# Retention in front of two expert layers: row stores on ScalarE's queue, eight load buffers, query scaling ahead of key scaling, and the first tile's turn behind the second tile's scores

## The chip, the cores and the metric

The kernel runs on one core of a Trainium2 chip, as one program. The metric is the device time of one execution in microseconds, and the time of a kernel is the median of its runs. The profiles are made by the hardware profiler during one execution.

## What is computed

Three layers follow each other, all in float32. The first is retention: causal scores with a decay for each head, no softmax. The second routes each of 2304 tokens to one of 8 experts with a fixed capacity, in the order of the logits over all tokens and experts. The third is a dense layer whose gate is h * tanh(softplus(h)).

```python
scores = scale * np.matmul(q, k.transpose(0, 1, 3, 2))      # 4 batches, 8 heads, 576 rows, 64
ret = scores * Dmat[None, :, :, :]                          # gamma[h] ** (i - j) below the diagonal
x = np.matmul(ret, v)                                       # -> 2304 rows x 512
logits = x @ w_gate
for idx in np.argsort(-logits.flatten()):                   # greedy, capacity 2304 // 8 a expert
...
out[mask] = np.maximum(x[mask] @ w1[e], 0.0) @ w2[e]
h = out @ w_in
g = h * np.tanh(np.log1p(np.exp(np.minimum(h, 20.0))))
return g @ w_out
```

## The kernel before

**Retention** (`attention`, lines 133 to 334) goes through 18 tiles of 128 rows, four and a half tiles a batch. It computes the sum over earlier rows in chunks: within a tile by masked scores, between tiles by a running state of 64 x 64 a head. For each tile t there are seven steps, each a small function:

- `load` (L163) brings two blocks of 512 KB from HBM: `qk` (queries and keys, transposed) and `kv` (keys and values by rows). It is issued on SP's queue into the pool `ld`, which has six buffers of each.
- `scale` (L175) makes `ks` (keys times decay, L181) and then `qs` (queries times decay, L185), on GpSimd (POOL), but for tile 0, whose `ks` VectorE makes. In tiles 4 and 13, where a new batch begins in mid-tile, `qs` is a kept tile `qz`.
- `scores` (L187): 16 matmuls into two of three PSUM banks, then VectorE multiplies by the mask (`am`, L198).
- `carried` (L214): the product of state `S` and `qs` (L223) into the bank pair `pT`.
- `outputs` (L226): values times masked scores (L232) into the same pair; ScalarE (ACT) copies it to `xT` in two halves (L236).
- `state` (L200): adds `ks` times values to the running state in PSUM (L209); VectorE makes `S` for the next tile (L212).
- `turn` (L238): TensorE (PE) transposes `xT` against a tile that holds the identity and the gate's weights (L246), so that rows and logits come out together; VectorE adds up the logits `L` (L248), ACT copies the rows to `xs` (L250), and a DMA on SP's queue stores them to the scratch tensor `x` (L252), 256 KB a tile.

The order of PE, VectorE and POOL is the order in which the code is written (`manual_schedule`, L147). SP's and ACT's instructions are put in order by the framework's scheduler. It also gives each DMA of SP's and ACT's queues one of eight counters, `DMAHW0` to `DMAHW7`, in turn; a DMA waits, before it is issued, until the last DMA on its own counter has landed.

The first two tiles are written by hand (L278 to L294): scores(0), then for tile 0 carried, outputs, state, turn, scores(1), and for tile 1 scores(2), carried, outputs, state, turn, state(2). The loop from L295 takes two tiles o and b = o + 1 a round: scores(b), carried(o), carried(b), scores(b + 1), the scaling of the tiles two to four ahead, outputs(o), state(b), outputs(b), state(b + 1), turn(o), turn(b). When the last logits are there, routing begins with the counts `pF` (L331).

**After retention**, an order of work planned by `run_tasks` (L715) covers the rest: routing finds one expert after the other with its tokens by a search over the logits' bits, SP loads that expert's weights by the number found (`eid`), POOL gathers its rows of `x` by indirect DMA (L646), PE runs the expert (L810), and the dense layer follows in six tiles of 384 tokens (L1033, L1094). Nothing of this is touched by the change.

Of the kernel before, what the change touches and what calls it, by code (L numbers as in the profile page):

```python
# [7 lines left out]
F32 = mybir.dt.float32  # L8
# [5 lines left out]
ALU = mybir.AluOpType  # L14
# [3 lines left out]
P = 128  # L18
B, H, S, D = 4, 8, 576, 64
# [109 lines left out]
class Kernel:  # L129
# [3 lines left out]
    def attention(self):  # L133
        tc, nc, a = self.tc, self.nc, self.a
# [5 lines left out]
        self.ident = persist.tile([P, P], F32, name="ident")  # L140
        self.L = L = persist.tile([P, NT, E], F32, name="L")
        with ExitStack() as st:
            ld = st.enter_context(tc.tile_pool(name="ld", bufs=6))
            wk = st.enter_context(tc.tile_pool(name="wk", bufs=4))
            one = st.enter_context(tc.tile_pool(name="one", bufs=1))
            ps = st.enter_context(tc.tile_pool(name="ps", bufs=1, space=PSUM))
# [4 lines left out]
            gks = dec[:, DC["gk"]].rearrange("p (t h) -> p t h", h=H)  # L151
# [9 lines left out]
            QK, KV, QS, KS, AM, XT, PT, Sb = {}, {}, {}, {}, {}, {}, {}, {}  # L161
# [10 lines left out]
            def starts(t):  # L172
                return (t * P) % S == 0

            def scale(t, eng, keys=True, queries=True):  # L175

                if t >= NT:
                    return
                if keys and not starts(t + 1):
                    KS[t] = wk.tile([P, H, D], F32, name="ks")  # L180
                    eng.tensor_tensor(KS[t], KV[t][:, 0], gks[:, t, :, None].to_broadcast([P, H, D]), op=ALU.mult)  # L181
                if queries and not starts(t):
                    n = 64 if t in STRADDLE else P
                    QS[t] = QZ[t] if t in STRADDLE else wk.tile([P, HP, P], F32, name="qs")
                    eng.tensor_tensor(QS[t][:, :, :n], QK[t][:, 0, :, :n], gqs.rearrange("p (h i) -> p h i", i=P)[:, :, :n], op=ALU.mult)  # L185

            def scores(t):  # L187
                if t >= NT:
                    return
                into = [pA[(2 * t + i) % 3] for i in range(2)]  # L190
                for hp in range(HP):
                    for i in range(2):
                        sl = slice(i * 64, i * 64 + 64)
                        for o in (slice(0, 64), slice(64, P)):
                            nc.tensor.matmul(into[i][o, hp, :], QK[t][sl, 1, hp, o], QK[t][sl, 0, hp, :], start=True, stop=True)
                AM[t] = wk.tile([P, 2, HP, P], F32, name="am")
                for i in range(2):
                    nc.vector.tensor_tensor(AM[t][:, i], into[i], masks[t in STRADDLE][:, i], op=ALU.mult)  # L198

            def state(t):  # L200

                if starts(t + 1):
                    return
                s1 = ((t + 1) * P - 1) % S
                begin = s1 < P
                lo = P - 1 - s1 if begin else 0
                for h in range(H):
                    o = slice(h % 2 * 64, h % 2 * 64 + 64)
                    nc.tensor.matmul(pS[o, h // 2, :], KS[t][lo:, h, :], KV[t][lo:, 1, h, :],  # L209
                                     start=(begin and h < 2), stop=False, skip_group_check=True)  # L210
                Sb[t + 1] = wk.tile([P, HP, D], F32, name="S")
                nc.vector.tensor_tensor(Sb[t + 1], pS, gss[:, t + 1, :, None].to_broadcast([P, HP, D]), op=ALU.mult)  # L212

            def carried(t):  # L214

                PT[t] = ps.tile([P, 2, 512], F32, name="pT", bufs=2)[:, :, :2 * P].rearrange("p i (k j) -> p i k j", k=2)
                if starts(t):
                    return
                for k in range(2):
                    for i in range(2):  # L220
                        sl = slice(i * 64, i * 64 + 64)
                        for q in range(2):
                            nc.tensor.matmul(PT[t][q * 64:q * 64 + 64, i, k, :], Sb[t][sl, 2 * k + q, :], QS[t][sl, 2 * k + q, :],  # L223
                                             start=(k == 0), stop=False, skip_group_check=True)

            def outputs(t):  # L226

                first = starts(t)
                for i in range(2):
                    for k in range(2):  # L230
                        for q in range(2):
                            nc.tensor.matmul(PT[t][q * 64:q * 64 + 64, i, k, :], KV[t][:, 1, 4 * k + 2 * q + i, :], AM[t][:, i, 2 * k + q, :],  # L232
                                             start=(first and k == 0), stop=(k == 1), skip_group_check=True)
                XT[t] = wk.tile([P, HP, P], F32, name="xT")
                for i in range(2):
                    nc.scalar.copy(XT[t][:, 2 * i:2 * i + 2], PT[t][:, i])  # L236

            def turn(t):  # L238

                if t < 0:  # L240
                    return
                xs = wk.tile([P, DM], F32, name="xs")
                pX = ps.tile([P, 2, 512], F32, name="pX", tag="pT", bufs=2)
                for i in range(2):
                    for k in range(2):
                        nc.tensor.matmul(pX[:, i, k * P:k * P + P + E], XT[t][:, 2 * i + k, :], both[:, i, E - k * E:P + 2 * E - k * E],  # L246
                                         start=(k == 0), stop=(k == 1), skip_group_check=True)
                nc.vector.tensor_reduce(L[:, t, :], pX[:, :, P:P + E].rearrange("p i e -> p e i"), AX.X, ALU.add)  # L248
                for i in range(2):
                    nc.scalar.copy(xs.rearrange("p (k q i d) -> p i k q d", q=2, i=2, d=D)[:, i],  # L250
                                   pX[:, i, :2 * P + 2 * E].rearrange("p (k c) -> p k c", k=2)[:, :, :P].rearrange("p k (q d) -> p k q d", d=D))
                nc.sync.dma_start(a["x"][t * P:(t + 1) * P, :], xs)  # L252

            warm = one.tile([P, 512], BF16, name="warm")
            nc.vector.memset(warm, 0.0)
# [21 lines left out]
            nc.sync.dma_start(self.tri, a["tri"])  # L277
            scores(0)  # L278
            scale(0, nc.vector)
            scale(1, nc.gpsimd)  # L280
            scale(2, nc.gpsimd)
            for t in range(2):
                scale(t + 3, nc.gpsimd, queries=t == 0)
                if t:
                    scores(t + 1)
                carried(t)
                outputs(t)
                state(t)
                if t != 1:
                    turn(max(t - 1, 0))  # L290
                if t == 0:
                    scores(1)
            turn(t)
            state(t + 1)  # L294
            for o in range(2, NT, 2):  # L295
                b = o + 1
                load(o + 3)
# [25 lines left out]
            t = b  # L323
# [832 lines left out]
```

## Time and profile before

| | |
|---|---|
| time, median of 3 runs | 793.49 us (793.35 to 793.95) |
| the profiled execution | 789.16 us |
| its span, first to last instruction | 787.4 us |
| mean granted TensorE clock | 0.981 |
| PE, VectorE, POOL, ACT busy | 749.0, 671.5, 487.3, 406.1 us |
| retention, to the last instruction before the counts of routing | 0 to 83.1 us |
| bytes moved by DMA | 112.53 MB, of it 24.13 MB in the first 70 us |

The span is counted from the first to the last instruction; what lies around it, 1.8 us, belongs to the execution. The profiled execution is 4.3 us below the median of the runs. Windows and starts are in microseconds from the span's start. A DMA queue shows as SPq or ACTq: the instruction there only issues the transfer, and the landing comes later. "issue" as the reason of a wait means that the profile shows nothing for which the engine waited.

### The profile page before, as it was taken

The page shows a single profiled execution, that of the slowest core. Times are in us where ns is not written, and L with a number is a line of the kernel's source. Part 1 is how long each engine was busy: PE and PEld are TensorE (multiplying, and loading weights), DVE is VectorE, ACT ScalarE, POOL GpSimd, SP SyncE. Part 2 cuts the span into 40 slices and gives each one's busy share as a digit, 9 for nine tenths or more (in the row PEclk, how much of TensorE's full clock was granted, in tenths as well). Part 3 has the DMA queues.
Part 4 walks back from the last instruction along what each step waited for, and adds up shares of the span by engine and source line. Part 5 has one row for each costly group of instructions (what it writes and reads, how often), then busy time and mean ns, then how long its engine had stood idle before and what let it go on. Part 6 is the DMA issues. An engine that isn't in the chain of part 4 may idle for free.

```text
span 787.4 us, 16146 instructions
## 1 busy us (share of the span) xinstructions
PE 749.0 (95%) x6180; PEld 679.0 (86%) x6180; DVE 671.5 (85%) x1079; ACT 406.1 (52%) x781; POOL 487.3 (62%) x408
## 2 busy tenths in 40 slices
PE   7999479999999999899999999999999999999996
PEld 5889338999998999899988899899899899899894
DVE  3444787989888888777999999989999998999993
ACT  2223115657566575757764465556555545545442
POOL 5552036879798797430577586557656756756554
PEclk9999779999999999899999999999999999999999
DMA  9993165889888888986500011011001101000001
GB/s 341 406 397 117 46 215 192 272 278 306 273 299 274 288 293 265 342 290 210 174 22 21 1 51 30 1 41 31 11 1 51 31 1 41 21 1 27 14 1 40
DMA packets 61405, 112.53 MB, mean 143 GB/s; under 512 B 4880, under 2 KB 33296, under 8 KB 61328
## 3 DMA queue, kind: packets, MB, share of 16 engines
q1 hardware_dynamic: 45104, 74.01, 27.5%
q10 hardware_dynamic: 13248, 28.06, 10.4%
q0 software_dynamic: 2976, 9.44, 3.6%
q8 instruction: 48, 0.79, 0.4%
q14 instruction: 29, 0.24, 0.1%
HBM read 88.94 MB, written 22.54 MB: 142 GB/s over the span
## 4 chain that ended last, share of the span: by engine, by line
PE 38%; DVE 17%; POOL 3%; DMA 2%; issue 2%; ACT 2%; POOLq 0%; SPq 0%; ACTq 0%; DVEq 0%
PE mmc L1033 15%; PE po L1094 15%; DVE q L1063 9%; DVE n L1058 5%; PE mma L810 4%; PE mmb L810 3%; DVE n L1068 2%; DMA st<-w 1%; ACT whi L597 1%; POOL gl L1075 1%; DVE wlo L600 1%; POOL n L1065 1%; DMA q<-y_scratch 1%; POOL out L1108 1%; DMA yt<-y_scratch 0%
## 5 line engine op out<-in xcount | busy, mean ns | idle before, releaser
L1063 DVE RECIPROCAL q<-q 128x384 f32<-128x384 f32 x96 | 243.8, 2540 | 0.0
L1065 POOL TENSOR_TENSOR n<-n,q 128x384 f32<-128x384 f32 x96 | 100.9, 1051 | 161.6 <-DVE q L1063 153.7
L600 POOL TENSOR_TENSOR wlo<-st,whi 128x1024 fp32r<-128x1024 f32 x51 | 122.6, 2417 | 16.5 <-ACT whi L597 12.2
L1033 PE MATMUL mmc<-yh,whi 128*128 128x384 f32 x384 | 129.9, 338 | 0.8 <-DVE n L1068 0.8
L1033 PE MATMUL mmc<-yh,wlo 128*128 128x384 f32 x384 | 129.9, 338 | 0.0
L1033 PE MATMUL mmc<-yl,whi 128*128 128x384 f32 x384 | 129.8, 338 | 0.1
L1075 POOL TENSOR_TENSOR gl<-n,gh 128x384 fp32r<-128x384 f32 x96 | 120.0, 1252 | 3.6 <-ACT gh L1073 3.5
L1073 ACT CAST gh<-n 128x384 fp32r<-128x384 f32 x96 | 49.3, 514 | 141.0 <-DVE n L1068 140.5
L1058 DVE SCALAR_TENSOR_TENSOR n<-s 128x384 f32<-128x384 f32 x96 | 114.7, 1197 | 5.1 <-POOL gl L1075 3.9
L1094 PE MATMUL po<-whi,gl 128*128 128x512 f32 x288 | 113.9, 395 | 0.7 <-POOL gl L1075 0.4
L1094 PE MATMUL po<-whi,gh 128*128 128x512 f32 x288 | 114.4, 397 | 0.2 <-ACT gh L1073 0.2
L1094 PE MATMUL po<-wlo,gh 128*128 128x512 f32 x288 | 114.1, 396 | 0.0
L597 ACT CAST whi<-st 128x1024 fp32r<-128x1024 f32 x80 | 82.7, 1044 | 33.8 <-DMA st<-w 28.1
L810 PE MATMUL mma<-xh,whi 128*128 128x288 f32 x256 | 78.5, 307 | 2.9 <-ACT xh L657 2.6
L810 PE MATMUL mma<-xl,whi 128*128 128x288 f32 x256 | 77.5, 303 | 1.7 <-DVE xl L659 1.7
L810 PE MATMUL mmb<-hl,whi 128*128 128x288 f32 x256 | 77.3, 302 | 0.0
L810 PE MATMUL mmb<-hh,whi 128*128 128x288 f32 x256 | 77.3, 302 | 0.0
L810 PE MATMUL mma<-xh,wlo 128*128 128x288 f32 x256 | 76.9, 301 | 0.0
L1033 PEld LDWEIGHTS mmc<-yh,whi 128*128 128x128 f32 x384 | 72.1, 188 | 5.2 <-DVE n L1068 1.2
L810 PE MATMUL mmb<-hh,wlo 128*128 128x288 f32 x256 | 75.9, 297 | 0.0
L1033 PEld LDWEIGHTS mmc<-yl,whi 128*128 128x128 f32 x384 | 72.1, 188 | 4.1 <-DVE yl L993 0.3
L1033 PEld LDWEIGHTS mmc<-yh,wlo 128*128 128x128 f32 x384 | 72.0, 188 | 0.0
(152 smaller groups left out, 1546.9 us busy)
## 6 DMA issues: line engine op xcount, KB each, us to landing
st<-w SPq DMA_DIRECT2D x64, 512.0 KB, 6.0
qk<-qk SPq DMA_DIRECT2D x18, 512.0 KB, 8.0
kv<-kv SPq DMA_DIRECT2D x18, 512.0 KB, 8.7
std<-w_out ACTq DMA_DIRECT2D x15, 512.0 KB, 4.9
std<-w_in ACTq DMA_DIRECT2D x14, 512.0 KB, 5.6
x_scratch<-xs SPq DMA_DIRECT2D x18, 256.0 KB, 5.6
y_scratch<-y ACTq DMA_DIRECT2D x32, 144.0 KB, 4.2
yt<-y_scratch SPq DMA_DIRECT2D x22, 192.0 KB, 2.4
```

Of the source, the lines that this page charges most:

```text
L597: self.nc.scalar.copy(dst[0], st)
L600: (self.nc.vector if lo.engine == DVE else self.nc.gpsimd).tensor_tensor(dst[1], st, dst[0].bitcast(F32), op=ALU.subtract)
L810: self.nc.tensor.matmul(bank[1][:, :CAP], al if h == 2 else ah, bl if h == 1 else bh, start=(first and j == h == 0), stop=(last and j == n ...
L1033: self.nc.tensor.matmul(bank[1][:, :TILE], (wl if h == 2 else wh)[:, c, cs], x[c][h == 1], start=(c == h == 0), stop=(c == HP - 1 and h == 2))
L1058: v.scalar_tensor_tensor(u, s, 2.0, s, op0=ALU.subtract, op1=ALU.mult)
L1063: v.reciprocal(q, q)
L1065: nc.gpsimd.tensor_tensor(u, u, q, op=ALU.mult)
L1068: v.tensor_tensor(u, u, p, op=ALU.mult)
L1073: nc.scalar.copy(gh, u)
L1075: nc.gpsimd.tensor_tensor(gl, u, gh.bitcast(F32), op=ALU.subtract)
L1094: nc.tensor.matmul(po[j], (gl if h == 2 else gh)[:, js], (wl if h == 1 else wh)[:, f % 2], start=(f == h == 0), stop=(f == DFF // P - 1 an ...
L1108: d = nc.gpsimd.indirect_dma_start(out=self.a["out"], out_offset=bass.IndirectOffsetOnAxis(ap=self.tok[:, t * 3 + j:t * 3 + j + 1], axis=0 ...
```

## The change

Four edits, all in `attention`: the pool `ld` has eight buffers of each kind; `scale` makes `qs` ahead of `ks`; the store of `xs` is issued on ACT's queue; and the first two tiles are written out with scores(1) ahead of turn(0), carried(1) ahead of scores(2), and the scaling of tile 3 ahead of tile 0's steps.

```diff
-            ld = st.enter_context(tc.tile_pool(name="ld", bufs=6))
+            ld = st.enter_context(tc.tile_pool(name="ld", bufs=8))
...
-                if keys and not starts(t + 1):
-                    KS[t] = wk.tile([P, H, D], F32, name="ks")
-                    eng.tensor_tensor(KS[t], KV[t][:, 0], gks[:, t, :, None].to_broadcast([P, H, D]), op=ALU.mult)
                 if queries and not starts(t):
                     n = 64 if t in STRADDLE else P
                     QS[t] = QZ[t] if t in STRADDLE else wk.tile([P, HP, P], F32, name="qs")
                     eng.tensor_tensor(QS[t][:, :, :n], QK[t][:, 0, :, :n], gqs.rearrange("p (h i) -> p h i", i=P)[:, :, :n], op=ALU.mult)
+                if keys and not starts(t + 1):
+                    KS[t] = wk.tile([P, H, D], F32, name="ks")
+                    eng.tensor_tensor(KS[t], KV[t][:, 0], gks[:, t, :, None].to_broadcast([P, H, D]), op=ALU.mult)
...
-                nc.sync.dma_start(a["x"][t * P:(t + 1) * P, :], xs)
+                nc.scalar.dma_start(a["x"][t * P:(t + 1) * P, :], xs)
...
-            for t in range(2):
-                scale(t + 3, nc.gpsimd, queries=t == 0)
-                if t:
-                    scores(t + 1)
-                carried(t)
-                outputs(t)
-                state(t)
-                if t != 1:
-                    turn(max(t - 1, 0))
-                if t == 0:
-                    scores(1)
-            turn(t)
-            state(t + 1)
+            scale(3, nc.gpsimd)
+            carried(0)
+            outputs(0)
+            state(0)
+            scale(4, nc.gpsimd, queries=False)
+            scores(1)
+            turn(0)
+            carried(1)
+            scores(2)
+            outputs(1)
+            state(1)
+            turn(1)
+            state(2)
```

What this makes of the engines' order is seen at three places. The numbers behind the names are those of the buffers; in brackets stand the counters for which a row waits before it is issued. On SP's queue, from the identity on: `qk_314`, `kv_316` are tile 5, `qk_318`, `kv_320` tile 6, `qk_447`, `kv_449` tile 7, `qk_451` is tile 8. Before:

```order
L275 DMA ident_65<-ident 128x128 [waits DMAHW7_49]
L277 DMA tri_157<-tri 128x128 [waits DMAHW0_49]
L167 DMA qk_314<-qk 128x1024 [waits DMAHW1_49]
L170 DMA kv_316<-kv 128x1024 [waits DMAHW2_49]
L167 DMA qk_318<-qk 128x1024 [waits DMAHW3_49,PE_49]
L367 DMA rc_643<-rconsts 128x211 [waits DMAHW4_49]
L369 DMA ic_645<-iconsts 128x194 [waits DMAHW5_49]
L170 DMA kv_320<-kv 128x1024 [waits DMAHW6_49,DVE_49,PE_49]
L252 DMA x_scratch<-xs_214 128x512 [waits DMAHW7_49,Activation_49]
L167 DMA qk_447<-qk 128x1024 [waits DMAHW0_49,PE_49,Pool_49]
L167 DMA qk_451<-qk 128x1024 [waits DMAHW1_49,PE_49,Pool_49]
```

And in the change:

```order
L275 DMA ident_65<-ident 128x128 [waits DMAHW7_49]
L277 DMA tri_157<-tri 128x128 [waits DMAHW0_49]
L167 DMA qk_314<-qk 128x1024 [waits DMAHW1_49]
L170 DMA kv_316<-kv 128x1024 [waits DMAHW2_49]
L167 DMA qk_318<-qk 128x1024 [waits DMAHW3_49]
L170 DMA kv_320<-kv 128x1024 [waits DMAHW4_49]
L167 DMA qk_447<-qk 128x1024 [waits DMAHW5_49]
L170 DMA kv_449<-kv 128x1024 [waits DMAHW6_49]
L167 DMA qk_451<-qk 128x1024 [waits DMAHW7_49,PE_49]
L367 DMA rc_643<-rconsts 128x211 [waits DMAHW0_49]
L369 DMA ic_645<-iconsts 128x194 [waits DMAHW1_49]
```

The loads of tiles 6 and 7 now wait for no engine, only for their own counter, and stand two places further ahead; `kv_320` has taken counter 4 and `qk_451` counter 7. On ACT, the first tiles before (`xT_201`, `xs_214` are tile 0, `xT_281`, `xs_294` tile 1, `xT_393` is tile 2):

```order
L236 COPY xT_201<-pT_192 128x256 [waits PE_49]
L236 COPY xT_201<-pT_192 128x256
L250 COPY xs_214<-pX_215 128x4x64 [waits DVE_49]
L250 COPY xs_214<-pX_215 128x4x64
L236 COPY xT_281<-pT_264 128x256 [waits PE_49]
L236 COPY xT_281<-pT_264 128x256
L250 COPY xs_294<-pX_295 128x4x64 [waits DVE_49]
L250 COPY xs_294<-pX_295 128x4x64
L236 COPY xT_393<-pT_341 128x256 [waits PE_49]
```

And in the change (`xs_235` is now tile 0):

```order
L236 COPY xT_201<-pT_192 128x256 [waits PE_49]
L236 COPY xT_201<-pT_192 128x256
L250 COPY xs_235<-pX_236 128x4x64 [waits DVE_49]
L250 COPY xs_235<-pX_236 128x4x64
L252 DMA x_scratch<-xs_235 128x512 [waits DMAHW4_49,Activation_49]
L236 COPY xT_281<-pT_245 128x256 [waits PE_49]
L236 COPY xT_281<-pT_245 128x256
L250 COPY xs_294<-pX_295 128x4x64 [waits DVE_49]
L250 COPY xs_294<-pX_295 128x4x64
L252 DMA x_scratch<-xs_294 128x512 [waits DMAHW7_49,Activation_49]
L236 COPY xT_393<-pT_341 128x256 [waits PE_49]
```

The stores of tiles 0 and 1 now stand in ACT's stream ahead of the next tile's `xT` copies, on counters 4 and 7; the number for which the first one waits, 48, is reached when the third DMA on counter 4 has landed (16 a DMA), and that is `kv_320`; the second one's third on counter 7 is `qk_451`. On POOL, tiles 1 to 3 in the change, where every pair has changed places (before, each `ks` stood ahead of its `qs`):

```order
L182 TENSOR_TENSOR qs_180<-qk_137,gq_82 128x512 [waits DMAHW7_49,DMAHW4_49]
L185 TENSOR_TENSOR ks_182<-kv_140,dec_81 128x512 [waits DMAHW6_49,DMAHW3_49]
L182 TENSOR_TENSOR qs_184<-qk_143,gq_82 128x512 [waits DMAHW0_49]
L185 TENSOR_TENSOR ks_186<-kv_145,dec_81 128x512 [waits DMAHW1_49]
L182 TENSOR_TENSOR qs_188<-qk_147,gq_82 128x512 [waits DMAHW2_49]
L185 TENSOR_TENSOR ks_190<-kv_149,dec_81 128x512 [waits DMAHW3_49]
```

A `qs` so waits for the `qk` load alone and no longer for the `kv` load behind it. In the change's rows L182 is the query scaling and L185 the key scaling.

## Rows read from the trace of the kernel before

**Rows 1.** The page: span.

```profile
span 787.4 us, 16146 instructions
```

**Rows 2.** Windows: length, PE, PEld, DVE, ACT, POOL busy, PE clock, DMA share, GB/s.

```profile
13.10:83.10 70.00, 66.15 (x1416) 60.78 (x1416) 33.21 (x72) 20.64 (x64) 32.35 (x30) 1.00 0.78 302
83.10:108.00 24.90, 12.06 (x157) 6.71 (x155) 18.89 (x80) 1.34 (x5) 0.00 (x0) 0.66 0.17 58
```

**Rows 3.** Waits of PE, 13 to 84 us: total, times, longest.

```profile
PE pA L195 <- issue: 1.8, 2, 1.0
PE pT L223 <- POOL qs L185: 1.2, 1, 1.2
PE pA L195 <- DMA qk<-qk: 0.9, 1, 0.9
PE pT L232 <- issue: 0.6, 1, 0.6
```

**Rows 4.** Timeline of PE: turn(1), and the first counts of routing.

```profile
16.19 1.20 PE L246 MATMUL pX<-both,xT 128*128 128x136 f32 x8
...
83.11 0.53 PE L331 MATMUL pF<-oh,G 128*128 128x8 bf16 x15
```

**Rows 5.** Timeline of SP's queue, 17.5 to 27 us: issues.

```profile
18.32 0.33 SPq L167 DMA_DIRECT2D qk<-qk  x1
19.53 0.33 SPq L367 DMA_DIRECT2D rc<-rconsts  x1
...
22.20 0.33 SPq L170 DMA_DIRECT2D kv<-kv  x1
```

**Rows 6.** DMA issues, 18.2 to 19 us: size, microseconds to landing.

```profile
qk<-qk SPq DMA_DIRECT2D x1, 512.0 KB, 8.1
```

**Rows 7.** DMA, 20 to 50 us: packets, bytes, rate.

```profile
DMA packets 4265, 12.28 MB, mean 409 GB/s; under 512 B 476, under 2 KB 890, under 8 KB 4260
```

**Rows 8.** Tile kv, all its loads.

```profile
DMA to landing us min/median/max: 4.4/8.7/10.9
```

**Rows 9.** Timeline of ACT, 8.9 to 18.2 us: start, length, what, idle before.

```profile
11.43 0.65 ACT L250 COPY xs<-pX 128x256 f32<-128x256 f32 x2 [1.80 <-DVE L L248]
15.77 0.65 ACT L236 COPY xT<-pT 128x256 f32<-128x256 f32 x2 [3.69 <-PE pT L232]
```

**Rows 10.** Timeline of ACT, 144.5 to 146 us: a store's issue.

```profile
144.68 0.33 ACTq L846 DMA_DIRECT2D y_scratch<-y  x1
```

**Rows 11.** Timeline of ACT, 68.8 to 71 us: a round's second row copy.

```profile
69.91 0.65 ACT L250 COPY xs<-pX 128x256 f32<-128x256 f32 x2 [0.28 <-ACT xs L250]
```

**Rows 12.** Windows of PE: length, busy, granted clock, DMA share, GB/s.

```profile
85.00:87.90 2.90, 0.20 (x2) 1.00 0.38 143
87.90:100.90 13.00, 4.07 (x96) 0.50 0.00 1
100.90:104.90 4.00, 4.00 (x12) 0.50 0.00 2
105.00:108.00 3.00, 2.94 (x30) 1.00 0.90 298
```

**Rows 13.** The same, of the 128x512 matmul of L820 alone.

```profile
101.00:104.90 3.90, 3.90 (x10) 0.50 0.00 2
110.70:112.40 1.70, 1.70 (x8) 1.00 1.08 385
```

**Rows 14.** Timeline of POOL, 9 to 16.5 us.

```profile
11.32 1.04 POOL L181 TENSOR_TENSOR ks<-kv,dec 128x512 f32<-128x512 f32 x1 [5.23 <-DMA kv<-kv]
12.32 1.27 POOL L185 TENSOR_TENSOR qs<-qk,gq 128x512 f32<-128x512 f32 x1
```

**Rows 15.** DMA issues, 4.2 to 4.5 us.

```profile
gq<-decays SPq DMA_DIRECT2D x1, 256.0 KB, 7.5
```

**Rows 16.** Window at the longest PE wait named issue; columns as in rows 2.

```profile
29.60:30.70 1.10, 0.14 (x5) 0.00 (x0) 0.00 (x0) 0.00 (x0) 1.03 (x1) 1.00 1.00 398
```

**Rows 17.** Waits of SP's queue, 0 to 85 us: total, times, longest.

```profile
SPq L252 <- ACT xs L250: 24.8, 10, 6.7
```

## The prediction

> **What bounds the kernel now.** I read the page first, for the span [rows 1], then busy times by stage, since the change touches retention alone, then the waits of the engine that the stage shows as full, then single starts. From 13.1 to 83.1 us PE is busy 66.15 of 70.00 us, while the DMA engines move data for 0.78 of it, the granted clock is 1.00, and no other engine is half busy (PEld are PE's own weight loads) [rows 2]. So retention is bound by PE, though it looks like a stage of loads. The waits confirm it: in those 70 us PE waits 4.5 us in all, 0.9 for a load (tile 2's queries and keys, once, at the start), 1.2 for POOL's `qs`, and 1.8 + 0.6 = 2.4 for nothing that the profile names [rows 3]. After 83.1 us the picture changes: PE is busy 12.06 of 24.90 us [rows 2], because routing is a chain of small steps between VectorE and PE. That chain starts with the counts `pF` at 83.11 [rows 4], and the weights of the first expert are loaded by the number it finds. Nothing behind it can start without it, so I move the whole rest of the program by what `pF` moves. A profiled execution of this kernel took 789.16 us, 1.8 more than its span [rows 1] and 4.3 less than the median, 793.49; I work out a difference on the trace and add it to the median.
>
> **Stores on ACT's queue.** This is the term that decides. The store of tile 0 now stands in ACT's own stream, and the copies of tile 1 behind it. In the order of the change it waits for counter 4 to reach its third landing, and that is the load of `kv` of tile 6. Before, the store waited on SP's queue and held loads only; those were early enough for PE.
>
> When does that load land? It can be issued when the second DMA on counter 4, the `qk` of tile 4, has landed. Before, the next DMA on that counter was `rc`, issued at 19.53 [rows 5]; I take 19.5 for `kv`, which stood at 22.20. The `qk` ahead of it in the queue was issued at 18.32 [rows 5] and took 8.1 us [rows 6], so it landed at 26.4. The `kv` behind it is 0.524 MB, at the 409 GB/s of this stretch [rows 7] 1.3 us more: 27.7. As a check, 19.5 plus the median of all `kv` loads, 8.7 [rows 8], is 28.2. The bounds are that row's extremes, 4.4 and 10.9: landings at 23.9 and 30.4.
>
> ACT copied tile 0's rows from 11.43 to 12.08 [rows 9]; with tile 1's scores now ahead of the turn I expect about 13. From there it would stand still until 27.7. Then it issues the store (0.33 us, as the `y_scratch` store does [rows 10]) and makes tile 1's `xT` from 28.0 on. Before, that copy began at 15.77 [rows 9]: **12.2 us late**. PE's turn(1), which began at 16.19 [rows 4], 0.4 us behind that copy's start, needs it, and PE takes its work in order: state(2), scores(3) and all later tiles stand behind turn(1), though their loads have landed. PE has no idle time after that from which to win the loss back, but for the other waits of [rows 3], 1.2 + 2.4 us. Bounds from the landings: 8.4 and 14.9 us.
>
> The store of tile 1 waits likewise for `qk` of tile 8. Its own load, the two before it and the first store, 1.83 MB, come in between, so at 409 GB/s it lands some 4.5 us after 27.7, at 32.2; ACT reaches the store at about 31 and is next needed by outputs(2), not before 34. I cost it at nothing; its cover is those 3 us. In the change's order the stores of tiles 3 to 10 each wait for a load too, one that SP may issue a round of two tiles or more before that store is due: nothing as well, and a rival below if that fails.
>
> The other 17 issues lie on ACT at 0.33 us each [rows 10]. ACT is busy 20.64 of 70 us [rows 2]. An issue falls between two tiles' row copies, where ACT idles 0.28 us anyway [rows 11], so the second copy is 0.05 us late, and PE reads that bank half a microsecond later: nothing. If that cover is gone, 8 rounds of 0.33 us are 2.6.
>
> The Trainium skill (DMA: Bandwidth & Descriptors, section Issuing engines are not separate DMA queues) says that DMAs of all issuing engines run on the same 16 DMA engines, and that a second issuing engine saves no more than the issue time. By it this edit would be worth nothing, neither gain nor loss, and the sum would be the POOL term alone, about 792. The rule is about transfers; it says nothing of what stands behind a waiting issue in the issuing engine's own stream.
>
> **What the hold does to the clock.** PE would be idle from about 16.3 to 28.4. The row for that is the start of routing: after 85.0 PE does 0.20 us of work in 2.90, and from 87.9 the granted clock is 0.50, the 1.2 GHz level. It stays there until PE has worked without a gap from 100.9 to 104.9 [rows 12]. So I expect about 4 us at the lower level after turn(1). The price: one and the same matmul runs 10 times in 3.90 us at 0.50 and 8 times in 1.70 at 1.00 [rows 13], 0.39 against 0.21, so 45% of 4 us: **1.8 us lost**. Bounds: 0 (it does not fall), and 2.7 (6 us at that level).
>
> **Query scaling first.** The 1.2 us that PE waits for `qs` of tile 3 [rows 3] go: POOL now makes it ahead of `ks`, whose load lands later. **1.2 us won**, the whole row, since the hold leaves POOL 10 us more in any case. State(1) and the following need `ks` one scaling (1.27 us [rows 14]) later, long before PE gets there.
>
> **The turned start.** Scores(1) can begin 1.2 us earlier, the length of a turn [rows 4], since turn(0) no longer stands ahead of it. But carried(1) now comes ahead of scores(2) and needs `qs` of tile 1, which needs `gq`: issued at 4.29, it took 7.5 us [rows 15], 11.8, and the scaling takes 1.27 [rows 14]. So carried(1) begins at 13.1, where scores(2) had to wait for its load anyway [rows 3]. Then the same two steps follow in the other order, and turn(1) would be due where it was. I take 0; between -0.5 and +0.5.
>
> **Eight buffers.** Loads may run two tiles further ahead, and PE waits for none of them now: 0 by themselves. But PE, late by 12 us, frees buffers late, so that the DMA queue is less full in the second half. PE's waits named "issue" are 2.4 us in three places [rows 3]; at the longest, 29.6 to 30.7 us, PE and ACT and VectorE stand still with the DMA engines at 1.00 and 398 GB/s [rows 16]. If the full queue is their cause, the emptier one ends some of them. I take half as gone: **1.2 us won**, between 0 and 2.4.
>
> **The sum:** 12.2 + 1.8 - 1.2 - 1.2 = 11.6 us. `pF` would start at 94.7, the profiled execution would take 800.8, and the median 793.5 + 11.6 = 805.1, which I give as **805**. From no change this kernel's runs can tell about 0.2%, or 1.6 us.
>
> **The rivals.** (a) *Less is lost*: the hold comes, but the clock stays up and all waits named "issue" go: 12.2 - 1.2 - 2.4 = 8.6, so 802.1; if the load also lands at 23.9, 798.3. For it speaks that the lower clock came after sparse work of another kind; against it, that PE has nothing at all to do in the hold. 0.14. (b) *The hold comes back*: later loads now wait for PE to free buffers, and the eight stores of tiles 3 to 10 meet them late. If four come 1 us beyond their cover, 4 us more: 809. It decides where a load lands less than 3 us before the next `xT`. Against it: the order puts a round between them. 0.13. (c) *Not slower*: a DMA issue waits beside ACT's stream, and not in it, so that no copy is held. Then the POOL term alone is left, 1.2 us: 792.3, and with the "issue" waits gone too 789.9. It decides at whether tile 1's `xT` starts before 17 us. Against it speaks SP, where an issue that waits for ACT's row copies holds SP's stream for 24.8 us in 10 places, up to 6.7 at a time [rows 17]; no row shows ACT in such a wait. The rule of the Trainium skill quoted above (DMA: Bandwidth & Descriptors, Issuing engines are not separate DMA queues) lands here too, at 792. 0.08, half of it within 0.2%, half faster.
>
> **How the numbers follow.** The forecast has 0.65, and with (a) and (b) slower comes to 0.92; same 0.04, faster 0.04. The forecast's own range is 801 to 808 (landings half-way to their bounds, clock and waits at either end). With most of (a) and (b) it is 799.5 to 810, which leaves out (c), the low end of (a) and the tail of (b).
>
> **What would show it.** In the changed kernel's trace: on ACT a gap of about 15 us ahead of tile 1's `xT`, which starts near 28; turn(1) on PE right behind it, with 12 us of idle PE before; the clock at 0.5 in the slice around 20 to 33 us; no wait of L223 for POOL; `pF` near 94.7, and the rest as before, shifted. I am wrong if ACT's copies of tile 1 start before 17 us, if PE wins more than 5 us back between turn(1) and `pF`, or if what follows routing does not shift by what `pF` does.

## Result: 1.4% slower, as forecast, by a hold of 12 us on ScalarE

| | before | changed |
|---|---|---|
| median of four runs, us | 793.44 | 804.83 |
| runs, us | 793.35 to 793.95 | 803.79 to 805.96 |
| ratio to before, 95% interval | | 1.014 [1.0125, 1.0155] |
| profiled execution, us | 789.16 | 805.96 |
| start of `pF`, us | 83.11 | 93.31 |

In three later sets of comparisons, each on a chip of its own, the kernel before has another median: 793.58, 793.96 and 788.68. So a time is compared within its set alone, by its ratio. The changed kernel, taken again, gives 804.28 and 1.0128 [1.0111, 1.0146].

The page of the changed kernel, as [rows 1]:

```profile
span 804.2 us, 16124 instructions
```

Windows, as [rows 2] and [rows 12] (length, PE, PEld, DVE, ACT, POOL busy, clock, DMA share, GB/s); first retention and the start of routing, then four pieces of retention's beginning:

```profile
13.10:93.30 80.20, 67.64 (x1416) 63.24 (x1416) 32.78 (x71) 20.89 (x65) 33.30 (x31) 0.91 0.72 264
93.30:118.00 24.70, 11.67 (x152) 6.56 (x152) 18.70 (x79) 1.29 (x4) 0.00 (x0) 0.59 0.15 47
...
13.00:21.10 8.10, 3.03 (x80) 2.72 (x80) 1.71 (x3) 0.30 (x2) 5.90 (x6) 1.00 1.03 402
21.20:28.50 7.30, 0.00 (x0) 0.00 (x0) 0.00 (x0) 0.38 (x2) 3.98 (x4) 0.50 1.03 409
28.50:34.70 6.20, 6.15 (x80) 5.79 (x84) 1.57 (x4) 0.92 (x3) 2.31 (x3) 0.50 1.05 407
34.80:42.00 7.20, 7.20 (x160) 6.66 (x156) 2.71 (x7) 2.50 (x8) 4.42 (x4) 1.00 1.00 371
```

The first of the four pieces in the kernel before:

```profile
13.00:21.10 8.10, 6.78 (x168) 6.03 (x172) 4.15 (x8) 1.29 (x4) 5.13 (x5) 1.00 1.04 406
```

The stage has grown from 70.0 to 80.2 us with the same 1416 matmuls; the first steps of routing behind it keep their distances (the first matmul of L514, at 100.88 us before, is 10.21 us late). All of the loss lies in the first three of the four pieces: up to 21.1 PE works for 3.03 us where it worked for 6.78, from 21.2 to 28.5 it does nothing while the DMA engines are full (share 1.03, the loads come at the rate they had), and from 28.5 to 34.7 it is busy throughout but at a granted clock of 0.50, the 1.2 GHz level. From 34.8 on it is full at 1.00.

What holds PE, from the waits of PE between 13 and 94 us, as [rows 3]:

```profile
PE pX L246 <- ACT xT L236: 12.1, 1, 12.1
PE pT L223 <- POOL qs L182: 1.1, 1, 1.1
```

One wait of 12.1 us for ScalarE has come; the load wait, the wait for tile 3's `qs` and all three named "issue" have gone. (The 1.1 us is another `qs`, tile 1's, at 13.4.) What holds ScalarE, from its timeline, as [rows 9]:

```profile
12.65 0.65 ACT L250 COPY xs<-pX 128x256 f32<-128x256 f32 x2 [2.41 <-DVE L L248]
27.74 0.34 ACTq L252 DMA_DIRECT2D x_scratch<-xs  x1
28.12 0.65 ACT L236 COPY xT<-pT 128x256 f32<-128x256 f32 x2 [14.83 <-DMA kv<-kv]
30.98 0.65 ACT L250 COPY xs<-pX 128x256 f32<-128x256 f32 x2 [2.21 <-DVE L L248]
31.65 0.33 ACTq L252 DMA_DIRECT2D x_scratch<-xs  x1
```

Tile 0's rows are copied by 13.3, but the store's issue comes at 27.74, and tile 1's `xT` right behind it, after 14.83 us in which ScalarE does nothing. The profile names a load of `kv` as the releaser: of tile 6, the third on counter 4. The second store is issued as soon as its copies are done (31.65). On PE turn(1) and `pF`, as [rows 4]:

```profile
28.55 2.18 PE L246 MATMUL pX<-both,xT 128*128 128x136 f32 x8 [12.10 <-ACT xT L236]
...
93.31 0.53 PE L331 MATMUL pF<-oh,G 128*128 128x8 bf16 x15
```

turn(1) is 12.36 us late and takes 2.18 us instead of 1.20, at the lower clock; `pF` is 10.20 us late. In between, the same work has won 2.2 us back, the lower clock already taken off.

### The profile page after: what moved, and what is told of

Its sections match the earlier page's. It is cut to its first block, busy times and chain, and to the rows that moved or that the text cites. A ratio compares the mean times of both kernels' runs of the same rounds, so it can differ in the third digit from the quotient of the medians.

```text
span 804.2 us, 16124 instructions
## 1 busy us (share of the span) xinstructions
PE 750.8 (93%) x6176; PEld 681.4 (85%) x6180; DVE 671.4 (83%) x1079; ACT 406.9 (51%) x781; POOL 487.7 (61%) x408
## 4 chain that ended last, share of the span: by engine, by line
PE 37%; DVE 16%; issue 4%; ACT 2%; DMA 2%; POOL 2%; ACTq 0%; POOLq 0%; SPq 0%; DVEq 0%
PE mmc L1033 15%; PE po L1094 15%; DVE q L1063 8%; DVE n L1058 5%; PE mma L810 4%; PE mmb L810 3%; DVE n L1068 2%; DMA st<-w 1%; ACT whi L597 1%; DVE wlo L600 1%; DMA yt<-y_scratch 1%; POOL gl L1075 1%; POOL n L1065 1%; POOL out L1108 0%; DVE words L776 0%
```

## Experiments

The theory (H): ScalarE stands at a DMA issue that waits for a load, and the kernel loses as long as that lasts, plus the lower clock behind it, less the short waits that a PE with a full supply no longer meets. The rivals: the stores disturb the loads (Q); another of the four edits costs the time (R).

### The two kernels side by side

No edit; the kernel before and the changed one once more, on one chip.

> The kernel before, unchanged, for a second profiled execution beside those of the changed kernel. In the two profiles at hand pF moves by 10.2 us, but the end of the program by 16.8, while the medians differ by 11.3. If the growth behind pF is only a difference of executions (the profiled one of before is 4.3 us below its own median), this profile and the next one of the changed kernel should have their expert stages within 2 us of each other. If the change itself costs something behind routing, the stage from pF to the end is again 5 to 7 us longer in the changed kernel than here.

> The changed kernel, unchanged. Ratio to before 1.0125 to 1.0155 again. Theory H (ACT stands at tile 0's store until a load has landed): xT of tile 1 again starts within 1.5 us of 28.1, right behind that issue, turn(1) on PE half a microsecond later, and PE has no wait over 1 us from there to pF. Rival Q (the stores on a second queue disturb the loads): PE's loss would be spread over many waits for loads.

Timeline of PE, turn(1) and `pF`, of the kernel before:

```profile
16.63 1.19 PE L246 MATMUL pX<-both,xT 128*128 128x136 f32 x8
...
82.86 0.53 PE L331 MATMUL pF<-oh,G 128*128 128x8 bf16 x15
```

And of the changed one:

```profile
28.51 2.18 PE L246 MATMUL pX<-both,xT 128*128 128x136 f32 x8 [11.85 <-ACT xT L236]
...
93.30 0.53 PE L331 MATMUL pF<-oh,G 128*128 128x8 bf16 x15
```

H's picture is the same to a tenth of a microsecond. Q falls: the loss stands in one wait. And `pF` is 10.4 us later here, the span 8.0 (801.2 against 793.2), the ratio 1.0128, some 10.2 us. The growth behind `pF` in the first pair of profiles was no work of the change: the profile of before there was of an execution that takes 6.0 us less from `pF` to the end than this one, in the same kernel. (Here that stretch is 2.4 us shorter in the changed kernel than in the one before; I had expected the two within 2 us.)

### The stores back on SP

```diff
-                nc.scalar.dma_start(a["x"][t * P:(t + 1) * P, :], xs)
+                nc.sync.dma_start(a["x"][t * P:(t + 1) * P, :], xs)
```

> The changed kernel with the row stores back on SP's queue; the order of the scalings, the eight buffers and the order of the first tiles stay. Theory H: ACT is not held, xT of tile 1 starts before 17 us and turn(1) before 17.5, the clock stays at 1.0 from 21 to 35 us, and the time comes back to 791 to 797 us, a ratio of 0.997 to 1.005 (the won waits of 1.2 and up to 2.4 us against stores that now hold SP behind loads sent further ahead, up to 3). Rival R (the order of the first tiles or the deeper load queue costs the time, not the queue of the stores): turn(1) stays late and the ratio stays above 1.010.

795.07 us, 1.0015 [1.0005, 1.0025]. Timeline of ACT:

```profile
16.05 0.65 ACT L236 COPY xT<-pT 128x256 f32<-128x256 f32 x2 [2.98 <-PE pT L232]
...
38.85 0.65 ACT L250 COPY xs<-pX 128x256 f32<-128x256 f32 x2 [2.48 <-DVE am L198]
```

The hold is gone, turn(1) begins at 16.48, and nearly all of the loss is gone with it: the other three edits cost 0.15%, not 1.3%. R falls. But they win nothing either; the waits of PE say why:

```profile
PE pA L195 <- issue: 1.9, 2, 1.0
PE pT L232 <- issue: 1.4, 2, 0.8
PE pT L223 <- POOL ks L185: 1.3, 1, 1.3
```

The "issue" waits are all there again, and one put down to `ks` has come (it ends at 39.59 us). The work there, carried(7), does not read that `ks`, which is tile 9's. It needs the PSUM pair that tile 5's row copy empties, and that copy (38.85, above) ends at 39.50, 0.1 us before PE goes on. What held the copy is seen with the eight buffers alone, below. `pF` begins at 85.19, 2.3 us late.

### The store alone

The kernel before with that line on ScalarE's queue, and nothing else.

```diff
-                nc.sync.dma_start(a["x"][t * P:(t + 1) * P, :], xs)
+                nc.scalar.dma_start(a["x"][t * P:(t + 1) * P, :], xs)
```

> The kernel before with the row stores on ScalarE's queue and nothing else. Here the store of tile 0 waits, on its counter, for the load of ident, not for kv of tile 6; ident landed at 22.3 us in the profile of the changed kernel. Theory H (the loss is as long as the hold): the issue at 22 to 23, xT of tile 1 right behind it, turn(1) on PE at 22.7 to 23.7 instead of 16.2, so 7 us late; with the clock falling near 21 and a part of the waits named issue gone, pF 6.5 to 9 us later than before and a ratio of 1.007 to 1.0115. Rival Q (stores on a second queue cost, however long the hold): the ratio of the changed kernel, 1.0128. Rival N (the edit alone costs nothing, only its mixture with eight buffers does): below 1.002.

800.09 us, 1.0079 [1.0064, 1.0094], inside H's range. Timeline of ACT:

```profile
22.44 0.34 ACTq L252 DMA_DIRECT2D x_scratch<-xs  x1
22.82 0.65 ACT L236 COPY xT<-pT 128x256 f32<-128x256 f32 x2 [10.63 <-DMA ident<-ident]
```

The same line of code waits for another DMA here, because with six buffers fewer loads stand ahead of it in the order; the hold is 10.6 us instead of 14.8, turn(1) comes at 23.25, `pF` at 87.91, 4.8 to 5.1 us late by the two profiles of the kernel before; I had expected 6.5 to 9. The waits named "issue" are gone here too, with six buffers: it is the hold that takes them away, not the deeper supply of loads. And PE has no wait for `qs` either, though the keys are still scaled first.

### Filling the hold

The changed kernel with 50 matmuls of zeros in front of turn(1); nothing reads what they write.

```diff
+            for _ in range(50):
+                nc.tensor.matmul(pA[0].rearrange("p h i -> p (h i)"), warm[:, :P], warm, start=True, stop=True)
             turn(1)
```

> The changed kernel with 50 matmuls of zeros (128x512, bf16) on PE just ahead of turn(1), in the hold; nothing reads what they write. The hold itself stays: turn(1) still near 28.5. If the lower clock after the hold costs what the trace says (6.25 us at 0.50 behind turn(1)), the granted clock stays at 1.0 over the whole stretch from 16 to 35, pF starts 2 to 3 us earlier than in the changed kernel, and the time is 801.5 to 803, a ratio to before of 1.010 to 1.012. If the clock costs nothing there (waits behind it would have been as long), pF and the time stay within 0.7 us of the changed kernel's. If the filling work lasts beyond the hold, turn(1) comes later than 28.5 and the time grows by that.

802.35 us, 1.0109 [1.0092, 1.0126]. Timeline of PE (the added matmuls, turn(1), `pF`):

```profile
16.88 10.96 PE L294 MATMUL pA<-warm 128*128 128x512 bf16 x50
29.35 1.19 PE L246 MATMUL pX<-both,xT 128*128 128x136 f32 x8 [1.51 <-ACT xT L236]
...
91.34 0.53 PE L333 MATMUL pF<-oh,G 128*128 128x8 bf16 x15
```

Windows of it, over the stretch that was at 0.50 in the changed kernel:

```profile
21.20:28.50 7.30, 6.65 (x31) 2.84 (x29) 0.00 (x0) 0.00 (x0) 4.03 (x4) 1.00 1.03 407
28.50:34.70 6.20, 5.35 (x132) 4.98 (x134) 2.61 (x6) 1.29 (x4) 3.39 (x3) 1.00 1.04 406
```

The clock stays up and turn(1) takes 1.19 us again. ScalarE's hold ended 0.8 us later here (28.54; the load landed later, which I did not pursue), but from turn(1) to `pF` it takes 61.99 us instead of 64.79. So the lower clock costs 2.8 us. `pF` starts 2.0 us earlier, the 2.8 less those 0.8, and the medians are 1.9 us apart (1.0109 against 1.0128, though the intervals overlap).

### Queries first, alone

The kernel before with this edit of `scale` and nothing else: the three lines that make `ks` stand behind those that make `qs`.

```diff
-                if keys and not starts(t + 1):
-                    KS[t] = wk.tile([P, H, D], F32, name="ks")
-                    eng.tensor_tensor(KS[t], KV[t][:, 0], gks[:, t, :, None].to_broadcast([P, H, D]), op=ALU.mult)
...
+                if keys and not starts(t + 1):
+                    KS[t] = wk.tile([P, H, D], F32, name="ks")
+                    eng.tensor_tensor(KS[t], KV[t][:, 0], gks[:, t, :, None].to_broadcast([P, H, D]), op=ALU.mult)
```

> The kernel before with the queries scaled ahead of the keys and nothing else. If the term of the prediction holds, PE's wait of 1.2 us for qs of tile 3 goes and the time falls by about that: a ratio of 0.998 to 0.9992. If another wait takes its place (ks or a load comes last instead), the ratio is 1.000 within its interval.

793.18 us, 0.999 [0.998, 1.0001]: 0.8 us less, within the range for the whole 1.2 us and not clear of no change. The time does not decide, so I look at the waits of PE, 13 to 84 us:

```profile
PE pA L195 <- issue: 1.9, 2, 1.0
PE pT L232 <- issue: 1.2, 2, 0.8
PE pA L195 <- DMA qk<-qk: 1.0, 1, 1.0
```

The wait for `qs` is gone, but 0.8 us for "issue" at another place have come in (0.6 stood there before). Its place on PE's timeline:

```profile
23.78 0.87 PE L232 MATMUL pT<-am,kv 128*64 128x128 f32 x11 [0.83 <-issue]
```

The outputs of a tile stop after 5 of 16 matmuls; the profile shows no engine and no data for which they would wait. The DMA queues between 21.3 and 22.5 us (packets, MB, share):

```profile
q1 hardware_dynamic: 148, 0.48, 101.4%
q8 instruction: 1, 0.02, 5.8%
```

One packet of 16 KB of PE's instructions is among the data; the trace has it from 21.38 to 22.49, and PE goes on 1.3 us after its end. The two L195 waits of this run end at 30.82 and 56.25, and their packets at 29.43 and 54.84, 1.4 us before. I read this as PE waiting for its own instructions: with `qs` early, it merely reaches the end of them sooner. `pF` begins at 83.14, no earlier than in the two profiles of the kernel before (83.11 and 82.86).

The places bear this out. Counted from 0, the waits stand at PE's matmuls 348, 474, 599, 852 and 977. In every profile here that has waits named "issue" they stand, but for one, at these or at 725, to within one matmul: 125 to 127 matmuls apart, each with its weight load, at four different lines of the code.

### Eight buffers, alone

```diff
-            ld = st.enter_context(tc.tile_pool(name="ld", bufs=6))
+            ld = st.enter_context(tc.tile_pool(name="ld", bufs=8))
```

> The kernel before with eight load buffers and nothing else; the stores stay on SP. With the stores back on SP the changed kernel is 1.0015 of before, though PE's wait for qs of tile 3 is gone there: its pF stands 2.4 us later. If the deeper load queue is the cause (a load that PE needs stands behind stores and behind loads sent further ahead, as ks of tile 6 at 39.6 us), this kernel is slower than before by 2 to 4 us, a ratio of 1.0025 to 1.005, with PE waiting over 1 us for POOL near 39. If the order of the first tiles is the cause, this kernel is at 0.9995 to 1.001.

795.96 us, 1.0025 [1.0015, 1.0035], at the lower end of the range for the deeper queue. PE's waits for POOL:

```profile
PE pT L223 <- POOL ks L181: 1.4, 1, 1.4
PE pT L223 <- POOL qs L185: 1.3, 1, 1.3
```

And ScalarE waits for an old store to free a row buffer; with it, from PE's timeline, the wait of 1.4 us:

```profile
38.59 0.65 ACT L250 COPY xs<-pX 128x256 f32<-128x256 f32 x2 [2.20 <-DMA x_scratch<-xs]
39.33 0.67 PE L223 MATMUL pT<-qs,S 64*64 64x128 f32 x16 [1.44 <-POOL ks L181]
```

PE goes on 0.1 us after this copy's end at 39.24, as it did with the stores back on SP. In the kernel before that `ks` is later still (39.00 to 40.04 in its second profile), and carried(7) runs ahead of it there, from 37.8 us on, without a wait. So it is the copy, not `ks`, that holds PE, and the load that I expected to be late is not the cause. There are four row buffers, so tile 5's copy needs the one of tile 1; SP issues tile 1's store at 31.72, behind the loads now sent ahead, where it was 26.55 in the second profile of the kernel before.

`pF` begins at 85.17, as with the three edits together (85.19). So the buffers account for that delay of some 2 us; queries first and the turned start together add about nothing. The turned start was not run by itself.

### The first four stores on GpSimd

```diff
-                nc.scalar.dma_start(a["x"][t * P:(t + 1) * P, :], xs)
+                (nc.gpsimd if t < 4 else nc.scalar).dma_start(a["x"][t * P:(t + 1) * P, :], xs)
```

> The changed kernel with the row stores of tiles 0 to 3 on GpSimd's queue, whose counters no load uses; the others stay on ScalarE. So no store waits for a load while loads pile up at the start, and the stores stand neither on SP ahead of loads. Theory H: no hold, xT of tile 1 before 17 us, turn(1) before 17.5, and the time at or below before, a ratio of 0.995 to 1.0005; this is also the version that could beat both. If the queue of ScalarE is not the cause, turn(1) is late here too and the ratio stays above 1.010. If the hold only moves on (ScalarE stands at the store of tile 4, whose counter waits for a load sent far ahead), a gap of 1 to 4 us on ScalarE ahead of its next xT near 36 us, and a ratio of 1.001 to 1.006.

799.72 us, 1.0076 [1.0061, 1.009]: slower than I had for the first and the third case; the second, over 1.010, has a late turn(1), which is not there (16.68). It is the third case in its mechanism; timeline of ACT:

```profile
36.21 0.65 ACT L250 COPY xs<-pX 128x256 f32<-128x256 f32 x2 [1.09 <-DVE L L248]
41.45 0.34 ACTq L252 DMA_DIRECT2D x_scratch<-xs  x1
41.88 0.65 ACT L250 COPY xs<-pX 128x256 f32<-128x256 f32 x2 [5.02 <-DMA qk<-qk]
```

The first store left on ScalarE, tile 4's, waits 4.6 us for a load, and the second tile's copy with it, which has to empty the bank that PE needs next:

```profile
42.63 1.13 PE L223 MATMUL pT<-qs,S 64*64 64x128 f32 x16 [3.88 <-issue]
```

PE starts 0.1 us after that copy's end at 42.53, and the granted clock is 0.50 from 42.05 to 45.46. (Here "issue" is a wait that the profile could not name, and no instruction packet ended just before.) `pF` begins at 87.25, 4.1 to 4.4 us late, while the time is 5.8 us longer; the rest is open. The hold is not a matter of tile 0: it has come here too, where a store on ScalarE meets a load on its counter that has not landed.

### Stores in groups

Each row is still stored, but tiles 0 to 7 in one DMA behind tile 7, then 8 to 11, 12 to 15, 16 and 17.

```diff
+                lo, hi = spans[t]
+                if t == lo:
+                    XS[lo] = one.tile([P, hi - lo, DM], F32, name=f"x{lo}")
+                xs = XS[lo][:, t - lo]
...
-                nc.sync.dma_start(a["x"][t * P:(t + 1) * P, :], xs)
+                if t == hi - 1:
+                    nc.sync.dma_start(a["x"][lo * P:hi * P, :].rearrange("(t p) d -> p t d", p=P), XS[lo])
```

The first of three has this on SP, in the kernel with the queries first; the second on ScalarE, in the changed kernel; the third on ScalarE, in the first's.

> The kernel before with the queries scaled first and the row stores in groups, still on SP: the rows of tiles 0 to 7 in one DMA after tile 7, then 8 to 11, 12 to 15, 16 and 17; every row is still stored. With the queries first alone, PE's wait for qs went but one for nothing named (1.1 us at 23.8) came in its place, and each of these waits ends 1.3 to 1.5 us after a packet of 16 KB of the instruction queue. Theory F (these waits are for PE's own instructions, whose packets stand behind data on the DMA engines): with 2 MB of stores out of the way the loads catch up, the DMA share falls below 0.9 somewhere between 30 and 45 us, the waits after that point (49.7 and 56.3 us, 1.9 us together, perhaps that at 37.5) go, and pF starts 1.5 to 4 us earlier: a ratio of 0.995 to 0.998. Rival G (the waits belong to those instructions, whatever the DMA engines do): the same waits at the same instructions, and a ratio of 0.999 to 1.0005. The first waits, up to 31 us, stay by either.

> The changed kernel with the same groups of row stores, on ScalarE's queue: all four edits stay, but the first store is due after tile 7, when the load whose counter it shares has landed. Theory H (the hold alone made the change slow): xT of tile 1 before 17 us, turn(1) before 17.5, no gap over 2 us on ScalarE ahead of a copy, and a ratio of 0.995 to 0.999. If stores on ScalarE or the order of the first tiles cost by themselves, above 1.003.

> As the grouped stores on SP, but on ScalarE's queue: six buffers, the old order of the first tiles, the queries first. If only what a store waits for decides, and not the queue that it stands in, the same as on SP within 0.15%: 0.995 to 0.998. If ScalarE is still held at the first group (its counter waits for a load of tile 9, due to land near 42, the copies of tile 7 end near 44), it is up to 2 us slower than on SP.

791.00, 790.79 and 789.60 us where before had 788.68: 1.0026 [1.0014, 1.0038], 1.0033 [1.002, 1.0046], 1.002 [1.0006, 1.0033]. None wins; all three missed my ranges. What they tell apart holds all the same. With all four edits and the stores on ScalarE there is no hold any more; all that ScalarE waits for between 12 and 84 us is

```profile
ACT xT L236 <- PE pT L232: 37.4, 17, 4.4
ACT x L253 <- DVE L L251: 14.9, 17, 2.4
```

and turn(1) begins at 16.74, `pF` at 83.84. But 1.0033 is above the 1.003 that I had set for a cost of the stores on ScalarE, or of the order of the first tiles, by themselves. The queue is not it: the first and the third version differ in the queue alone, and by 0.0006, within their intervals. The second and the third differ in the eight buffers and the order of the first tiles too, and by 0.0013, within their intervals as well, so no cost of these shows either. What all three share is the grouping and the queries first.

The Trainium skill (DMA: Bandwidth & Descriptors, Issuing engines are not separate DMA queues) says that DMAs of all issuing engines run on the same 16 DMA engines, and that a second issuing engine saves only the issue time. Here the runs agree. They part from it where the issue waits in the stream of an engine that others need: with all four edits the single stores cost 1.1% more on ScalarE than on SP (1.0128 against 1.0015).

Why nothing was won is seen on SP's version. Waits of PE:

```profile
PE pA L195 <- issue: 3.4, 2, 2.5
PE pT L232 <- issue: 1.0, 1, 1.0
```

Windows of it:

```profile
40.00:45.00 5.00, 5.00 (x96) 4.70 (x96) 1.71 (x5) 2.59 (x8) 3.45 (x3) 1.00 1.00 378
54.30:57.10 2.80, 0.31 (x11) 0.07 (x4) 0.00 (x0) 0.00 (x0) 0.00 (x0) 1.00 1.03 407
57.60:61.00 3.40, 3.40 (x43) 3.40 (x43) 1.60 (x3) 0.65 (x2) 2.73 (x3) 0.51 0.64 193
```

The wait at 49.7 us is gone, as theory F had it. But the DMA share did not fall below 0.9 between 30 and 45 us (it is 1.00 from 40 to 45), and `pF` comes later, at 85.59. The 2 MB store is issued at 44.96, the loads behind it come in a burst with a share of 1.03, and in it the wait at matmul 977, 0.89 us with the queries first alone, has grown to 2.49 us. It ends at 57.08; the only packet of PE's instructions nearby ran from 54.65 to 55.59, 1.5 us before. Behind it the granted clock is 0.51 for 3.4 us, the lower level, which costs more. Neither theory stands as I wrote it. The places belong to the instructions, as G had it; whether PE waits there, and how long, changes with the transfers, as F had it. That the store's size made the long wait is argued, not shown: no other size was run. Of the 1.0033 of the second version `pF` shows about 1 us; where the rest lies is open.

## Why the prediction was right, and where it was not

I forecast 805 us with a range of 799.5 to 810; it is 804.83. That the two are this close is luck: the sum was 11.6 us at `pF`, and 10.2 to 10.4 were measured there, with two terms off by 1 us and more in opposite directions. (My inner range, 801 to 808, comes to 800 to 809 by the terms named for it.) The terms, on the three profiles of one chip (before, changed, changed with the hold filled):

| term | forecast, us | measured, us | from |
|---|---|---|---|
| hold (turn(1) late) | +12.2 | +11.9 | 28.51 - 16.63 |
| lower clock behind it | +1.8 | +2.8 | 64.79 - 61.99 |
| waits won back | -1.2 - 1.2 | -4.2 | 61.99 - 66.23 |
| `pF` | +11.6 | +10.4 | 93.30 - 82.86 |

- **The hold.** Right in mechanism and size, from the landing of the load: I had the issue at 27.7 and `xT` at 28.0, and they came at 27.74 and 28.12. The load itself was issued at 19.55, for my 19.5. That the landing came within 0.1 us of my 27.7 is more than the bounds of 23.9 and 30.4 promised; with the hold filled the same store is issued at 28.54. The store of tile 1 and the later ones cost nothing, as I took it: they are issued right behind their copies. That this was not safe, GpSimd's version shows: one young load on the counter, and 4.6 us are lost at tile 4. So (b) was a real rival with its condition not met.
- **The clock.** Right in kind, too small: I put 4 us at the lower level, by the 4.0 us of full work that it took in [rows 12]. It took 6.25 us, from 28.55 to 34.80; my price of 45% of those is 2.8, as measured. The bound of 6 us was the better guess.
- **Query scaling first.** Here a step was wrong: "1.2 us won, the whole row". Alone it brings nothing at `pF`, because PE then waits elsewhere, by the places for its instructions (its time, 0.999 [0.998, 1.0001], does not decide). In the changed kernel it had no say: with the hold POOL has 10 us more anyway, as the prediction itself noted, and the store alone, with the keys first, has no wait for `qs` either.
- **Eight buffers.** "0 by themselves" holds in the changed kernel, where PE waits for no load, but not in general: with the stores on SP they cost 2.0 us (1.0025). And I said that the emptier queue ends the waits named "issue", half of them. All went, but the store alone, with six buffers, ends them too. As I read it, the late PE has its instructions loaded when it comes to them: in the changed kernel's second profile a packet lands at 35.19 and PE comes to matmul 348 at 37.59; with the queries first alone one lands at 22.49 and PE waits for that matmul until 23.78. No run was made to show this.
- **The waits won back.** They are the term that was sized worst, 4.2 us for 2.4. The named waits behind turn(1) in the second profile of the kernel before, all gone with the hold, are 3.1 us of it (1.9 + 0.3 for "issue", 0.9 for `qs`). The other 1.1 us lie in PE's busy time, 62.0 us for the same 1336 matmuls instead of 63.15; why is open. This error and the 1.0 us of clock went against each other and left `pF` 1.2 us earlier than forecast in this pair, 1.4 in the first (93.31 against 94.7).
- **The turned start.** 0, and carried(1) at 13.42 against my 13.1: right as far as the difference of the runs above can tell. But "no wait of L223 for POOL" did not come true: carried(1) waits 1.1 us for tile 1's `qs`, in place of the load wait that scores(2) had there.
- **The rest as before, shifted.** By the letter, one of my signs of being wrong came: the end moved by 16.8 us in the first pair and by 8.0 in the second, `pF` by 10.2 and 10.4. Two executions of the kernel before differ by 6.0 us behind `pF`, so a single pair can't judge this. The medians, 11.4 and 10.7 us apart, fit a shift.
- **(c)**, a ScalarE that is not held, is excluded by every run with a store that meets a late load.

## What to carry to other kernels

Before a DMA issue moves to an engine that computes, look at what the issue has to wait for, its counter's last DMA included, and not only at its data: everything behind it in that engine's stream waits too, and the loss goes by the distance to that landing (turn(1) was 11.9 us late here), not by the 0.33 us of the issue. On a queue that carries nothing but DMAs the same wait can be free. And when one short wait of a saturated engine is removed, ask which comes next: here it was, by all signs, the engine's own instructions, and `pF` won nothing.

## What the runs showed that I had not expected

- **Waits named "issue" can be waits for instructions.** PE's instructions come over the same DMA engines as the data, in packets of 16 KB (queue q8: 48 packets, 0.79 MB on the whole page; 49 in the version with 50 matmuls more). From 13 to 60 us, with the DMA share at 1.02 in the kernel before, PE stands still at some of the places named above, 125 to 127 matmuls apart, for up to 1.0 us, and in the version with grouped stores on SP for 2.5. Of the 40 waits named "issue" over 0.15 us, between 13 and 84 us in all profiles here, 39 end 1.2 to 1.6 us after the end of such a packet; the other is the one of the GpSimd version at 42.63. The Trainium skill (Runtime: NRT & Kernel Launch, Instruction fetch mechanics) gives the same 16 KB, 256 instructions, on a queue of the engine's own, and calls the cost mostly hidden. The trace agrees on the size. It agrees on the rest from 60 us on, where the kernel before has no such wait, at a DMA share of 0.30 from 60 to 83 us and of 0.85 from 130 to 300 (where PE has 1746 matmuls in 170 us, against 941 in the 47 us up to 60); it does not from 13 to 60 us.
- **More buffers can be slower.** Eight instead of six, on their own, 1.0025: the loads sent further ahead stand in front of a row store, the store frees its row buffer late, and the copy that waits for the buffer holds a PSUM bank that PE needs.
- **A releaser that a profile names can be the wrong one.** Twice PE's wait was put down to `ks` on POOL, which its work did not need; what the work did need was a copy on ScalarE that ended 0.1 us before. So ask what the work reads and where it writes.
- **The same kernel takes 788.7 or 793.6 us** by the set it is measured in (each set has one chip, so the two can't be told apart); between the two profiles of the kernel before the difference builds up from 140 to 340 us, in the expert stage. A difference between two profiles has to be read against that before it is explained.
